# Attention, mixture of experts and GLU on one core: who makes the rests of the split weights, and where the first GLU conversions stand

## The chip, the core and the metric

The kernel runs on one core of a Trainium2 chip. The metric is the device time of one execution in microseconds; less is better. The engines of the core are TensorE (PE, with its weight loads as PEld), VectorE (DVE), ScalarE (ACT), GpSimd (POOL) and SyncE (SP, which here only issues transfers). Each has its own queue and works through it in order; they wait for each other by semaphores.

## The reference

Three stages, each on the output of the one before. 1536 tokens (2 sequences of 768, model width 512).

```python
# 1. attention: 8 heads of 64, a window of 128 keys and 4 sink keys
scores = where(is_sink | in_window, q @ k.T / sqrt(D), -1e9)
x = softmax(scores) @ v
# 2. mixture of 8 experts, one per token, at most 384 tokens each
logits = x @ w_gate
e = argmax(logits, axis=1);  g = softmax(logits)[n, e]
x[n] = g * (relu(x[n] @ w1[e]) @ w2[e])      # 0 where the expert was full
# 3. GLU, d_ff 1536
out = (sigmoid(x @ w_gate2) * (x @ w_val)) @ w_out
```

## The kernel before

Every product of stages 2 and 3 is made at float32 accuracy from two parts of each operand: a high part (the operand rounded to the PE's fp32r format) and a rest (operand minus high part). A product is then three matmuls: high by high, high by rest, rest by high. Weights arrive by DMA in one of four `stage` buffers of 128 x 2048 and are turned into a `pair` (high part and rest). For an expert's weights this is `split_w` (L127 to 132): ACT casts the high part (L131), an engine `eng` subtracts (L132, 128x1024). An expert has 8 such blocks. For the GLU the weights come as 18 blocks of 1 MB in a format of two interleaved words per element, every second column of the stage, which `conv_a` first turns into float32: ACT scales (L149), DVE does a shift and two merges (L150, L152, L156). Then `conv_b` makes the pair: ACT casts (L163), `eng` subtracts (L164). A block is converted in two halves of 128x512. There are 30 GLU loads, since not all 18 blocks fit at once.

The order of every engine's instructions is the order in which the code issues them (the schedule is manual).

Attention works on 12 tiles of 128 tokens and ends in a list of steps by hand (L618 to 627) for the last tile. In it `keep(n)` (L485 to 489) issues n matmuls whose product nobody reads, in a PSUM bank of pool `ps_v`; they keep PE running. `keep(8)` stands there ahead of `logits`, `keep(32)` (L632) behind the last count of tokens (L631). `place` forms a token's position in its expert (L438, L440, L447; its running count is L442 on POOL), `scatter` writes its row (L468).

`experts` goes over the 8 experts. Each has a main tile of 128 tokens (48 matmuls at L754 in four runs of 12, with transposes L725 and L764 and evacuations on ACT and DVE: xh L728 and xl, hr L758, hh L767 and hl L768, yr L773) and extra tiles (`more_tiles`) that run only when the expert has more than 128 or 256 tokens, under `tc.If` (L818, L820). In this data experts 0 and 7 have two extra tiles, 3 and 5 one, the others none. `split_next` splits one block of a later expert and issues the next load (SP, L124); of the 8 of an expert four rests are made by POOL (`G_`) and four by DVE (`V`). From the end of expert 1 to that of expert 6, `order_ids` (L682 to 684) has POOL issue two indirect scatters that write the order of the tokens to DRAM. At the end of expert 7, before its extra tiles, `whole` and `convert` make the first two GLU blocks; blocks 2 and 3 follow after the last `put_y` and the zeros of the unused columns of yh and yl (L893, L894).

`glu` works on three chunks of 512 tokens (the last one 416 wide here), each in 12 steps. Step t does, in order: `conv_a` of up to four half blocks, `up` (24 matmuls at L167 to L169 into two banks, ACT's sigmoid L961 after the first 12, DVE's product L962, gh by ACT L963, gl by DVE L965), `conv_b` of those half blocks and the loads that follow, and `down` of step t - 1 (12 matmuls into the accumulators, from gh and gl). Of the 28 half blocks that are left at the start, step 0 takes four and the next ones three each; those of the 12 reloaded blocks follow by the same rule in the last two chunks.

Of the kernel before, what the change touches and what calls it, by code (L numbers as in the profile page):

```python
# [1 line left out]

# [17 lines left out]
P = 128  # L20
# [5 lines left out]
def kernel(  # L26
# [145 lines left out]
    def attention():  # L172
        with ExitStack() as st:
# [87 lines left out]
            def scores(n):  # L261
# [7 lines left out]
                t = i % NT  # L269
                ps = [ps_s.tile([P, BW + P], F32, tag="s", name="s") for _ in range(4)]  # L270
                for p in range(2):
# [212 lines left out]

            def keep(n):  # L485

                idle = ps_v.tile([P, 512], F32, tag="pv", name="idle")
                for _ in range(n):
                    nc.tensor.matmul(idle, ones, ones.unsqueeze(1).to_broadcast([P, 4, P]), start=True, stop=True)
# [128 lines left out]
            for f, *a in (  # L618
                (recip, j, 1), (divide, j, 1, 0, D + E), (transposes, n - 1, 0), (turned, n - 1, 0),
                (transposes, n - 1, 1), (turned, n - 1, 1), (sink_T, i), (pv, n - 2), (sink_pv, n - 2),  # L620
                (logits, j), (best, j), (where, j), (onehot, j), (pv, n - 1),
                (gate, j, 0), (place, j), (gate, j, 1), (gate, j, 2), (scatter, j),
                (sink_pv, n - 1), (recip, i, 0), (recip, i, 1), (divide, i, 0, D, D + E), (divide, i, 1, D, D + E),
                (keep, 8), (logits, i), (divide, i, 0, 0, D), (best, i), (where, i), (onehot, i),
                (divide, i, 1, 0, D), (gate, i, 0), (gate, i, 1), (gate, i, 2), (place, i), (scatter, i),
            ):
                f(*a)
# [65 lines left out]
    def experts(yh, yl):  # L693
        with ExitStack() as st:
# [99 lines left out]

            def more_tiles(e):

                w1a, w1b, w2a, w2b = (weights(4 * e + x) for x in range(4))

                def one(j):
                    x = turn_x(xe[:, j - 1], 1)  # L800
                    u = bank(ps_u, 1)
                    go(products(u, x, w1a, True, True))
                    ra = relu(u)
                    u = bank(ps_u, 1)
                    b = products(u, x, w1b, True, True)
                    go(b[:6])
                    ha = turn_h(ra, 0)
                    go(b[6:])
                    rb = relu(u)
                    y = bank(ps_y, 1)  # L810
                    a = products(y, ha, w2a, True, False)
                    go(a[:6])
                    hb = turn_h(rb, 1)
                    go(a[6:])
                    go(products(y, hb, w2b, False, True))
                    return raw_y(y, 1)

                with tc.If(cnt_e[e] > P):  # L818
                    put_y(e, 1, one(1))
                    with tc.If(cnt_e[e] > 2 * P):  # L820
                        put_y(e, 2, one(2))

            V, G_ = nc.vector, nc.gpsimd
            xs = {0: load_x(0), 1: load_x(1)}
# [5 lines left out]
            for e in range(E):  # L830
                w1a, w1b, w2a, w2b = (weights(4 * e + j) for j in range(4))
                m = 8 * e
                if e:
                    load_x_next(e + 2)
                    load_more(e)
                    split_next(m + 2, G_)
                    split_next(m + 3, V)
# [3 lines left out]
                if e:  # L841
                    put_y(e - 1, 0, yr)
                    split_next(m + 4, G_)
                else:
# [14 lines left out]
                if e:  # L859
                    split_next(m + 6, G_)  # L860
                if e + 1 < E:
# [8 lines left out]
                if e:  # L870
                    split_next(m + 8, G_)
                    split_next(m + 9, V)
                elif e == 0:
                    cnt_e = counts([nc.tensor.engine, nc.scalar.engine, nc.vector.engine])
                go(products(y, hb, w2b, False, True))
                yr = raw_y(y, 0)
                if e == 0:
                    pi = order(hp)
                elif e < 7:
                    order_ids(pi, 2 * (e - 1), 2 * e)  # L880
                if e + 1 == E:
                    for g in range(2):
                        whole(g)
                        convert(g)
                more_tiles(e)
            load_ids()
# [7 lines left out]
            nc.vector.tensor_copy(out=yl[:, :, bass.ds(kept, P)], in_=z)  # L894
            for g in range(2, 4):
                whole(g)
                convert(g)

    def whole(q):
        for step in range(3):  # L900
            conv_a([(q, 0, 512), (q, 512, SUB)], step)

    def convert(q):
        for h in range(2):
            conv_b(q, q, h * 512, h * 512 + 512, nc.gpsimd)
        load_glu(q + 4, q)


    def glu(yh, yl):
        with ExitStack() as st:  # L910
# [105 lines left out]
            def run(t0, t1, w, half, before):  # L1016
# [6 lines left out]
                for t in range(t0, t1):  # L1023
                    pend = []
                    n, r = steps[t]
                    while half and len(pend) < 4:
                        x, h = half[0]
                        if todo[x][0] > n + 2 or len(pend) == 3 and todo[x][0] > n + 1:
                            break
# [6 lines left out]
                    for x, h in pend:  # L1036
                        conv_b(x % 4, todo[x][2], h * 512, h * 512 + 512, nc.gpsimd)
                        if h and x + 4 < len(todo):
# [130 lines left out]
```

## Time and profile before

| what | value |
|---|---|
| median of 3 runs | 703.72 us (701.37 to 704.37) |
| profiled execution | 700.3 us |
| its span in the trace | 698.6 us |
| PE busy | 620.9 us, 89% |
| DVE busy | 377.2 us, 54% |
| ACT busy | 305.8 us, 44% |
| POOL busy | 273.1 us, 39% |
| mean granted clock of PE | 0.958 |

Stages by the trace: attention to about 136 us, its tail and the order to about 150, experts to 376, GLU to the end. The shares are means over the whole span; what bounds a stage is read in that stage. The rows below are from the timelines (start, duration, engine, line, operation, what is written and read, count; in brackets the idle time of that engine just before and what ended it) and from tables over short windows. PE's durations of single matmuls overlap, so their distance is their cost.

### The profile page before, as it was taken

How to read it: one execution, taken by the hardware profiler on the slowest of the kernel's cores; microseconds unless marked ns; L12 is line 12 of the kernel's file. 1: busy time of each engine (PE TensorE's matmuls, PEld its weight loads, DVE VectorE, ACT ScalarE, POOL GpSimd, SP SyncE). 2: the span in 40 equal slices, each digit the busy share in tenths (PEclk: the TensorE clock that was granted, in tenths of full speed). 3: DMA queues.
4: the chain of work that ended last, by engine and by line, in shares of the span. 5: the costliest groups of instructions: out<-in, count | busy, mean ns of one | idle time of the engine just before them, and what ended most of it. 6: DMA issues, size and time to landing. Idle time of an engine off the chain costs nothing.

```text
span 698.6 us, 9497 instructions
## 1 busy us (share of the span) xinstructions
PE 620.9 (89%) x3316; PEld 504.7 (72%) x3316; DVE 377.2 (54%) x784; ACT 305.8 (44%) x590; POOL 273.1 (39%) x250
## 2 busy tenths in 40 slices
PE   7899899899896998999497688989999999799896
PEld 4888788757674776776376566767888887789784
DVE  2565655542177526547415999994217951128921
ACT  3567666512286546566323553452214521124321
POOL 3145867540079617638301543452102420203422
PEclk9999879999999999999799999999999999899998
DMA  6977966050067929729700444544001340101101
GB/s 161 296 216 249 318 177 202 21 192 33 0 195 256 241 96 273 240 64 227 284 1 7 164 136 176 181 142 161 30 31 40 141 182 4 44 20 61 61 0 66
DMA packets 43640, 94.09 MB, mean 135 GB/s; under 512 B 5664, under 2 KB 24352, under 8 KB 39728
## 3 DMA queue, kind: packets, MB, share of 16 engines
q1 hardware_dynamic: 41264, 87.10, 41.0%
q0 software_dynamic: 2304, 6.09, 2.3%
q8 instruction: 38, 0.62, 0.4%
q14 instruction: 34, 0.28, 0.1%
HBM read 82.63 MB, written 10.75 MB: 134 GB/s over the span
## 4 chain that ended last, share of the span: by engine, by line
PE 28%; issue 11%; DVE 8%; ACT 5%; POOL 1%; POOLq 0%; ACTq 0%; DVEq 0%
PE g L167 5%; PE g L168 5%; PE g L169 5%; PE u L754 5%; DVE stage L152 3%; DVE stage L156 3%; PE acc L167 3%; PE acc L169 3%; PE acc L168 3%; ACT stage L149 2%; ACT pair L163 2%; DVE g L962 1%; ACT gh L963 1%; DVE stage L150 0%; ACT g L961 0%
## 5 line engine op out<-in xcount | busy, mean ns | idle before, releaser
L164 POOL TENSOR_TENSOR pair<-stage,pair 128x512 fp32r<-128x512 f32 x60 | 88.3, 1499 | 179.1 <-ACT pair L163 139.9
L132 POOL TENSOR_TENSOR pair<-stage,pair 128x1024 fp32r<-128x1024 f32 x37 | 93.4, 2527 | 88.4 <-ACT pair L131 88.2
L167 PE MATMUL g<-yh,pair 128*128 128x512 f32 (+1 forms) x288 | 110.2, 383 | 7.9 <-issue 4.8
L168 PE MATMUL g<-yl,pair 128*128 128x512 f32 (+1 forms) x288 | 110.0, 382 | 0.0
L169 PE MATMUL g<-yh,pair 128*128 128x512 f32 (+1 forms) x288 | 109.7, 381 | 0.0
L754 PE MATMUL u<-pair,xh 128*128 128x512 f32 x224 | 64.6, 416 | 25.1 <-ACT xh L728 14.2
L963 ACT CAST gh<-g 128x512 fp32r<-128x512 f32 (+1 forms) x36 | 21.3, 593 | 131.6 <-DVE g L962 127.6
L962 DVE TENSOR_TENSOR g<-g,g 128x512 f32<-128x512 f32 (+1 forms) x36 | 23.4, 649 | 90.2 <-PE g L169 85.8
L754 PEld LDWEIGHTS u<-pair,xh 128*128 128x128 f32 x224 | 41.9, 196 | 38.6 <-ACT xh L728 15.9
L167 PE MATMUL acc<-pair,gh 128*128 128x512 f32 x132 | 53.9, 408 | 17.4 <-ACT gh L963 17.4
L132 DVE TENSOR_TENSOR pair<-stage,pair 128x1024 fp32r<-128x1024 f32 x27 | 59.1, 2187 | 17.0 <-ACT pair L131 16.7
L167 PEld LDWEIGHTS g<-yh,pair 128*128 128x128 f32 x288 | 55.1, 191 | 17.3 <-issue 5.2
L131 ACT CAST pair<-stage 128x1024 fp32r<-128x1024 f32 x64 | 65.3, 1050 | 4.2 <-PEq L818 2.5
L754 PE MATMUL u<-pair,hh 128*128 128x512 f32 x224 | 61.0, 400 | 1.6 <-ACT pair L131 1.4
L168 PEld LDWEIGHTS g<-yl,pair 128*128 128x128 f32 x288 | 55.2, 192 | 8.0
L169 PEld LDWEIGHTS g<-yh,pair 128*128 128x128 f32 x288 | 55.2, 192 | 7.8
L295 ACT ACTIVATE pt<-sc,neg 128x260 f32<-128x260 f32 (+1 forms) x96 | 44.6, 491 | 34.4 <-DVE neg L284 34.3
L152 DVE SCALAR_TENSOR_TENSOR stage<-stage 128x512 int32<-128x512 int32 x60 | 57.5, 1009 | 3.3 <-ACT stage L149 3.2
L150 DVE TENSOR_SCALAR stage<-stage 128x512 int32<-128x512 int32 x60 | 55.9, 987 | 0.0
L169 PE MATMUL acc<-pair,gl 128*128 128x512 f32 x132 | 53.9, 408 | 0.0
L168 PE MATMUL acc<-pair,gh 128*128 128x512 f32 x132 | 52.8, 400 | 0.0
L754 PEld LDWEIGHTS u<-pair,hh 128*128 128x128 f32 x224 | 40.8, 188 | 13.9 <-ACT pair L131 4.6
(157 smaller groups left out, 1034.6 us busy)
## 6 DMA issues: line engine op xcount, KB each, us to landing
stage<-in_we_dram SPq DMA_DIRECT2D x64, 512.0 KB, 6.5
stage<-in_wd_dram SPq DMA_DIRECT2D x30, 1024.0 KB, 4.9
vraw<-in_vr_dram SPq DMA_DIRECT2D x12, 288.0 KB, 6.4
vt<-in_vt_dram SPq DMA_DIRECT2D x12, 256.0 KB, 3.3
kraw<-in_kd_dram SPq DMA_DIRECT2D x22, 132.0 KB, 4.6
qraw<-in_qd_dram SPq DMA_DIRECT2D x22, 128.0 KB, 4.2
slots<-zero SPq DMA_DIRECT2D x1, 2048.0 KB, 9.3
xs<-slots SPq DMA_DIRECT2D x8, 256.0 KB, 4.4
```

The source lines that it names most:

```text
L131: nc.scalar.copy(out=t[:, 0], in_=raw)
L132: eng.tensor_sub(out=t[:, 1], in0=raw, in1=t[:, 0].bitcast(F32))
L150: nc.vector.tensor_scalar(out=l_, in0=l_, scalar1=29, scalar2=None, op0=ALU.logical_shift_right)
L152: nc.vector.scalar_tensor_tensor(out=l_, in0=h_, scalar=3, in1=l_, op0=ALU.logical_shift_left, op1=ALU.bitwise_or)
L164: eng.tensor_sub(out=slot[s][:, 1, n0:n1], in0=f, in1=h_.bitcast(F32))
L167: nc.tensor.matmul(ps, ah, bh, start=start, stop=False)
L168: nc.tensor.matmul(ps, ah, bl, start=False, stop=False)
L169: nc.tensor.matmul(ps, al, bh, start=False, stop=stop)
L295: nc.scalar.activation(out=pt_[i][:, h, :w], in_=scs_[n][j][:, :w], func=AF.Exp, scale=-1.0, bias=neg_[i][:, h:h + 1],)
L754: nc.tensor.matmul(ps, a, b, start=start, stop=stop)
L962: nc.vector.tensor_tensor(out=g, in0=g, in1=pss[1], op=ALU.mult)
L963: nc.scalar.copy(out=gh[:, :w], in_=g)
```

## The change

Four things change.

1. All rests of weights in the experts and the GLU are made by DVE; POOL keeps ten rests in attention, the zeros of yl, the scatters of the order and the output.
2. In expert 7 only GLU block 0 is converted ahead of the extra tiles. The halves of blocks 1 to 3 and the pair of block 1 are put between the operations of the extra tiles, one at a time, at four places of each tile, in the list `fills`; where an extra tile is not run, an Else branch does them. The pairs of blocks 2 and 3 follow the zeros as before. Blocks 4 and 5 are loaded earlier.
3. `keep(8)` ahead of `logits` becomes `keep(9)` directly behind the last `sink_pv`, writing to a bank of `ps_s`, where the scores were.
4. A GLU step takes at most three half blocks.

```diff
-            def keep(n):
-
-                idle = ps_v.tile([P, 512], F32, tag="pv", name="idle")
+            def keep(n, pool=None):
+
+                if pool is None:
+                    idle = ps_v.tile([P, 512], F32, tag="pv", name="idle")
+                else:
+                    idle = ps_s.tile([P, 512], F32, tag="s", name="idle")
...
-                (keep, 8), (logits, i), (divide, i, 0, 0, D), (best, i), (where, i), (onehot, i),
+                (sink_pv, n - 1), (keep, 9, ps_s), (recip, i, 0), (recip, i, 1),
...
-            def more_tiles(e):
+            def more_tiles(e, fills):
...
+                    def beside():
+                        for f in todo[:1]:
+                            f()
+                        del todo[:1]
+
                     x = turn_x(xe[:, j - 1], 1)
                     u = bank(ps_u, 1)
                     go(products(u, x, w1a, True, True))
+                    beside()
                     ra = relu(u)
...
+                n = 4 * (len(fills) + 1) // 8
+                with tc.If(cnt_e[e] > P) as more:
+                    put_y(e, 1, one(1, fills[:n]))
+                    with tc.If(cnt_e[e] > 2 * P) as most:
+                        put_y(e, 2, one(2, fills[n:]))
+                    if fills:
+                        with most.Else():
+                            rest(fills[n:])
+                if fills:
+                    with more.Else():
+                        rest(fills)
...
-                    split_next(m + 2, G_)
+                    split_next(m + 2, V)
...
+                fills = []
                 if e + 1 == E:
-                    for g in range(2):
-                        whole(g)
-                        convert(g)
-                more_tiles(e)
+                    whole(0, 0, SUB)
+                    convert(0)
+                    load_glu(4, 0)
+                    for q in range(1, 4):
+                        fills += [partial(whole, q, h * 512, h * 512 + 512) for h in range(2)]
+                        if q == 1:
+                            fills.append(partial(convert, 1))
+                more_tiles(e, fills)
+            load_glu(5, 1)
...
-                    while half and len(pend) < 4:
+                    while half and len(pend) < 3:
                         x, h = half[0]
-                        if todo[x][0] > n + 2 or len(pend) == 3 and todo[x][0] > n + 1:
+                        if todo[x][0] > n + 2:
                             break
...
-                        conv_b(x % 4, todo[x][2], h * 512, h * 512 + 512, nc.gpsimd)
+                        conv_b(x % 4, todo[x][2], h * 512, h * 512 + 512, nc.vector)
```

The order of instructions in the queues shows the moves. First DVE in a GLU step of the first chunk, before:

```order
L962 TENSOR_TENSOR g<-g,g_5041 128x512
L965 TENSOR_TENSOR gl<-g,gh 128x512
L150 TENSOR_SCALAR stage_82<-stage_82 128x512 x2
L150 TENSOR_SCALAR stage_83<-stage_83 128x512
L152 SCALAR_TENSOR_TENSOR stage_82<-stage_82 128x512 x2
L152 SCALAR_TENSOR_TENSOR stage_83<-stage_83 128x512
L156 SCALAR_TENSOR_TENSOR stage_82<-stage_82 128x512 x2
L156 SCALAR_TENSOR_TENSOR stage_83<-stage_83 128x512
L962 TENSOR_TENSOR g<-g,g_5096 128x512
```

And DVE in such a step after (L991 is the product, L994 the low part, L165 the rest, L151, L153 and L157 the conversion):

```order
L991 TENSOR_TENSOR g<-g,g_5078 128x512
L994 TENSOR_TENSOR gl<-g,gh 128x512
L165 TENSOR_TENSOR pair_88<-stage_80,pair_88 128x512 x2
L165 TENSOR_TENSOR pair_88<-stage_81,pair_88 128x512
L151 TENSOR_SCALAR stage_81<-stage_81 128x512
L151 TENSOR_SCALAR stage_82<-stage_82 128x512 x2
L153 SCALAR_TENSOR_TENSOR stage_81<-stage_81 128x512
L153 SCALAR_TENSOR_TENSOR stage_82<-stage_82 128x512 x2
L157 SCALAR_TENSOR_TENSOR stage_81<-stage_81 128x512
L157 SCALAR_TENSOR_TENSOR stage_82<-stage_82 128x512 x2
L991 TENSOR_TENSOR g<-g,g_5130 128x512
```

Three rests have come into the row between the low part and the next conversion.

ACT at the end of expert 7's main tile before, with the jump over the extra tiles and the cast of the first extra tile's xh:

```order
L773 COPY yr<-u 128x512
L149 ACTIVATE stage_80<-stage_80 128x512 x2
L163 CAST pair_86<-stage_80 128x512 x2
L149 ACTIVATE stage_81<-stage_81 128x512 x2
L163 CAST pair_86<-stage_81 128x512 x2
L818 COMPARE_AND_BRANCH
L728 CAST xh<-t 128x512
```

And after, into the first extra tile:

```order
L777 COPY yr<-u 128x512
L150 ACTIVATE stage_80<-stage_80 128x512 x2
L164 CAST pair_86<-stage_80 128x512 x2
L836 COMPARE_AND_BRANCH
L732 CAST xh<-t 128x512
L150 ACTIVATE stage_81<-stage_81 128x512
L762 ACTIVATE hr<-u 128x512
L771 CAST hh<-t 128x512
L150 ACTIVATE stage_81<-stage_81 128x512
L762 ACTIVATE hr<-u 128x512
L164 CAST pair_86<-stage_81 128x512 x2
L771 CAST hh<-t 128x512
```

The second block's four operations have moved from ahead of the jump to three places inside the tile.

POOL in the experts before, around the end of expert 1 (idsd is the order of the tokens in DRAM, pi where each goes):

```order
L132 TENSOR_TENSOR pair_84<-stage_81,pair_84 128x1024
L132 TENSOR_TENSOR pair_85<-stage_82,pair_85 128x1024
L132 TENSOR_TENSOR pair_86<-stage_83,pair_86 128x1024
L132 TENSOR_TENSOR pair_87<-stage_80,pair_87 128x1024
L684 DMA idsd<-ids_67,pi 1536x1 x2
L818 UNCONDITIONAL_BRANCH
L132 TENSOR_TENSOR pair_88<-stage_81,pair_88 128x1024
```

And POOL after, from the last work of attention on:

```order
L651 TENSOR_TENSOR tmp<-kd_2284,lower_66 128x64
L797 CAST yl<-zeros 128x1664 x4
L721 UNCONDITIONAL_BRANCH
L688 DMA idsd<-ids_67,pi 1536x1 x3
L836 UNCONDITIONAL_BRANCH
L721 UNCONDITIONAL_BRANCH
L688 DMA idsd<-ids_67,pi 1536x1 x9
```

With the rests gone, nothing is left between the twelve scatters of the order but jumps.

## Rows read from the trace of the kernel before

**Rows 1.** Window in GLU chunk 1: length, busy per engine, PE clock, DMA share, GB/s.

```profile
410.00:420.00 10.00, 8.77 (x38) 6.64 (x37) 9.32 (x12) 4.49 (x8) 4.55 (x4) 1.00 0.44 135
```

**Rows 2.** Timeline of DVE and POOL, one GLU step of chunk 1.

```profile
434.06 0.68 DVE L962 TENSOR_TENSOR g<-g,g 128x512 f32<-128x512 f32 x1
435.42 0.69 DVE L965 TENSOR_TENSOR gl<-g,gh 128x512 fp32r<-128x512 f32 x1 [0.68 <-ACT gh L963]
436.02 4.53 POOL L164 TENSOR_TENSOR pair<-stage,pair 128x512 fp32r<-128x512 f32 x3 [5.45 <-ACT pair L163]
436.02 3.36 DVE L150 TENSOR_SCALAR stage<-stage 128x512 int32<-128x512 int32 x3
439.31 3.00 DVE L152 SCALAR_TENSOR_TENSOR stage<-stage 128x512 int32<-128x512 int32 x3
442.23 1.89 DVE L156 SCALAR_TENSOR_TENSOR stage<-stage 128x512 int32<-128x512 int32 x3
444.03 0.68 DVE L962 TENSOR_TENSOR g<-g,g 128x512 f32<-128x512 f32 x1
```

**Rows 3.** DVE lines: shortest/median/longest in ns, first and last start in us.

```profile
L150 DVE TENSOR_SCALAR stage<-stage x60: 413/988/1559, 331.3 to 656.2; 128x512 int32<-128x512 int32 x60
L152 DVE SCALAR_TENSOR_TENSOR stage<-stage x60: 677/683/1803, 333.9 to 660.0; 128x512 int32<-128x512 int32 x60
L132 DVE TENSOR_TENSOR pair<-stage,pair x27: 1224/2089/3650, 195.1 to 329.3; 128x1024 fp32r<-128x1024 f32 x27
```

**Rows 4.** Timelines of DVE and PE at the start of the GLU.

```profile
375.66 0.43 DVE L894 CAST yl<-zeros 128x512 f32 x1
...
394.44 0.80 PE L167 MATMUL acc<-pair,gh 128*128 128x512 f32 x1 [5.35 <-ACT gh L963]
```

**Rows 5.** Timeline of ACT, sigmoids of GLU steps 10 and 11, and of chunk 3.

```profile
481.41 0.60 ACT L961 ACTIVATE g<-g 128x512 f32<-128x512 f32 x1 [2.60 <-PE g L169]
489.57 0.60 ACT L961 ACTIVATE g<-g 128x512 f32<-128x512 f32 x1 [4.09 <-PE g L169]
...
616.72 0.52 ACT L961 ACTIVATE g<-g 128x416 f32<-128x416 f32 x1 [3.58 <-PE g L169]
623.72 0.52 ACT L961 ACTIVATE g<-g 128x416 f32<-128x416 f32 x1 [3.59 <-PE g L169]
...
677.30 0.52 ACT L961 ACTIVATE g<-g 128x416 f32<-128x416 f32 x1 [3.59 <-PE g L169]
```

**Rows 6.** Timelines of ACT and PE around expert 7's first extra tile.

```profile
335.85 1.28 ACT L163 CAST pair<-stage 128x512 fp32r<-128x512 f32 x2 [1.39 <-DVE stage L156]
...
342.29 0.58 ACT L728 CAST xh<-t 128x512 fp32r<-128x512 f32 x1
342.92 2.07 PE L754 MATMUL u<-pair,xh 128*128 128x512 f32 x4 [9.77 <-ACT xh L728]
```

**Rows 7.** Timelines of PE and POOL, at starts of expert tiles.

```profile
206.36 1.15 PE L754 MATMUL u<-pair,xh 128*128 128x512 f32 x4 [0.15 <-PEq L818]
209.40 1.79 POOL L684 DMA_INDIRECT idsd<-ids,pi  x1 [0.30 <-issue]
213.64 1.19 PE L754 MATMUL u<-pair,xh 128*128 128x512 f32 x4 [1.41 <-POOL pair L132]
227.11 1.01 PE L754 MATMUL u<-pair,xh 128*128 128x512 f32 x2 [4.49 <-issue]
273.93 1.29 PE L754 MATMUL u<-pair,xh 128*128 128x512 f32 x4 [3.11 <-PEq L818]
```

**Rows 8.** Window behind a scatter, columns as in rows 1.

```profile
215.00:216.00 1.00, 1.00 (x7) 0.87 (x6) 1.00 (x1) 1.00 (x2) 0.92 (x1) 1.00 0.00 0
```

**Rows 9.** Timelines of PE and POOL at the end of attention.

```profile
138.03 3.38 PE L489 MATMUL idle<-ones 128*128 128x512 bf16 x8 [1.53 <-DVE x L385]
140.55 0.21 POOL L442 TENSOR_TENSOR acc<-acc,oh_all 128x8 bf16<-128x8 bf16 x1
141.32 7.24 PE L489 MATMUL idle<-ones 128*128 128x512 bf16 x32
```

More of the change, by code (lines that the diff above doesn't have):

```diff
@@ L1 @@
 from contextlib import ExitStack
+from functools import partial
 import concourse.bass as bass
@@ L269, in scores @@
                 t = i % NT
-                ps = [ps_s.tile([P, BW + P], F32, tag="s", name="s") for _ in range(4)]
+                ps = [ps_s.tile([P, 512], F32, tag="s", name="s")[:, :BW + P] for _ in range(4)]
                 for p in range(2):
@@ L622, in attention @@
                 (gate, j, 0), (place, j), (gate, j, 1), (gate, j, 2), (scatter, j),
-                (sink_pv, n - 1), (recip, i, 0), (recip, i, 1), (divide, i, 0, D, D + E), (divide, i, 1, D, D + E),
-                (keep, 8), (logits, i), (divide, i, 0, 0, D), (best, i), (where, i), (onehot, i),
+                (sink_pv, n - 1), (keep, 9, ps_s), (recip, i, 0), (recip, i, 1),
+                (divide, i, 0, D, D + E), (divide, i, 1, D, D + E), (logits, i), (divide, i, 0, 0, D), (best, i), (where, i), (onehot, i),
                 (divide, i, 1, 0, D), (gate, i, 0), (gate, i, 1), (gate, i, 2), (place, i), (scatter, i),
@@ L793, in zero_y, with one @@
                 nc.gpsimd.tensor_copy(out=yl[:, d], in_=z)
-            def more_tiles(e):
+            def more_tiles(e, fills):
                 w1a, w1b, w2a, w2b = (weights(4 * e + x) for x in range(4))
-                def one(j):
+                def one(j, todo):
+                    def beside():
+                        for f in todo[:1]:
+                            f()
+                        del todo[:1]
                     x = turn_x(xe[:, j - 1], 1)
@@ L807, in one @@
                     ha = turn_h(ra, 0)
+                    beside()
                     go(b[6:])
                     rb = relu(u)
+                    beside()
                     y = bank(ps_y, 1)
@@ L813, in one @@
                     hb = turn_h(rb, 1)
+                    beside()
                     go(a[6:])
@@ L816, in one, with rest @@
                     return raw_y(y, 1)
[L818 to L823, printed above, removed]
+                def rest(todo):
+                    for f in todo:
+                        f()
+                n = 4 * (len(fills) + 1) // 8
[9 more added lines that the diff above has]
+                        rest(fills)
+            V = nc.vector
             xs = {0: load_x(0), 1: load_x(1)}
@@ L842, in experts @@
                     put_y(e - 1, 0, yr)
-                    split_next(m + 4, G_)
+                    split_next(m + 4, V)
                 else:
@@ L859, in experts @@
                 if e:
-                    split_next(m + 6, G_)
+                    split_next(m + 6, V)
                 if e + 1 < E:
@@ L870, in experts @@
                 if e:
-                    split_next(m + 8, G_)
+                    split_next(m + 8, V)
                     split_next(m + 9, V)
@@ L894, in experts, with whole @@
             nc.vector.tensor_copy(out=yl[:, :, bass.ds(kept, P)], in_=z)
[L895 to L899, printed above, removed]
+            for q in range(2, 4):
+                convert(q)
+                load_glu(q + 4, q)
+    def whole(q, n0, n1):
         for step in range(3):
-            conv_a([(q, 0, 512), (q, 512, SUB)], step)
+            conv_a([(q, n, n + 512) for n in range(n0, n1, 512)], step)
     def convert(q):
         for h in range(2):
-            conv_b(q, q, h * 512, h * 512 + 512, nc.gpsimd)
-        load_glu(q + 4, q)
+            conv_b(q, q, h * 512, h * 512 + 512, nc.vector)
     def glu(yh, yl):
```

## The prediction

> **What bounds the kernel now.** I read the page's busy shares and 40 slices first. TensorE (PE) is busy for 89% of the span and its clock is close to full in most slices, so there is little to win except where it stands still, and I looked for those places with the timelines. They lie in three stretches.
>
> The GLU's first chunk is the largest. In ten of its microseconds PE is busy 8.77 and VectorE (DVE) 9.32, at a granted clock of 1.00 [rows 1]. One step there [rows 2] is a closed ring on DVE: its product L962 starts at 434.06 and again at 444.03, 9.97 us later, and between the two it is never idle except 0.68 us before L965. PE is not that slow: from step 10 on, with no half block left to convert, the sigmoid L961 starts at 481.41 and next at 489.57, so a full step (24 matmuls up, 12 down) takes 8.16 us, or 0.227 us a matmul [rows 5]. PE therefore loses 1.8 us a step as long as conversions run, 28 half blocks at three a step, some nine steps. In the ring the two conversion lines L150 and L152 take 3.3 and 2.9 us for three halves [rows 2]; over the whole run their shortest are 413 and 677 ns, the longest 1559 and 1803 [rows 3]. They are long exactly while GpSimd (POOL) makes its three rests at L164, 436.02 to 440.55; L156, which follows when POOL has finished, takes 0.60 a piece. I read that as POOL stretching DVE.
>
> The second place is the last expert: PE waits 9.77 us, to 342.92, for xh, which ScalarE (ACT) casts at 342.29 only after converting two GLU blocks [rows 6]. The third are waits of 0.15 to 4.49 us at the experts' ends [rows 7]. In chunk 2 I count no gain.
>
> **The change, part by part.** Sums are made on the profiled execution (700.3 us), which lies 3.4 below the median of the runs.
>
> *GLU, rests on DVE.* Removed: three L164 a step on POOL. Added on DVE, between the low part L965 and L150 of the next halves: three subtractions of 128x512. None is in the trace; the nearest is L965, the same operation and shape on DVE, 0.60 from its start to L150's [rows 2]. If L150 and L152 fall to what they take undisturbed, the ring is 1.36 (L962 to L965) + 0.60 + 3 x 0.60 rests + 3 x 0.41 + 3 x 0.60 + 3 x 0.60 = 8.6 us, against PE's 8.16. The bounds of a ring: 8.2, where PE sets it, and 9.97 + 1.80 = 11.8, where the stretch stays. I take 8.6, since L156, right behind in the same ring, already shows the undisturbed pace.
>
> What 8.6 costs depends on the slack at the start. Before, gh of step 0 came so late that PE waited 5.35 until 394.44; its second up was finished at 389.09 [rows 4]. Behind the zeros of yl (375.66 + 0.4, [rows 4]) DVE now has four rests (2.4) and three halves (4.8 by the costs above): 383.3, and with 0.8 for the rests' waits on ACT's casts L962 at about 384.1; gh is cast by 385.5, 3.6 before PE wants it. The ring falls back 0.44 a step over 9.3 steps, 4.1 in all. That is about the slack, so I count no wait. PE unhindered from 389.09 reaches the sigmoid of step 10 after 9 downs of 2.72, 8 ups of 5.44 and half an up, at 459.8; in the trace it starts at 481.41 [rows 5]. Gain **21.6**. In chunk 3 (416 columns) a step without a wait takes 7.00 (616.72 to 623.72), and the last 7 steps, 623.72 to 677.30, take 53.58 for 49.0 [rows 5]. There a ring of 8.3 to 8.6 is slower than PE by 1.3 to 1.6 a step, but over four steps with new halves only, which the steps ahead cover. Gain **4.6**, bounds 0 and 4.6.
>
> *Expert 7.* ACT converts block 0 alone ahead of the extra tiles; its two casts (1.28) start at 335.85, so xh can follow at 337.1 instead of 342.29 [rows 6]. Gain **5.1**. The six half blocks that go between the operations of two extra tiles take 1.6 us on DVE and 0.6 on ACT each. Each tile keeps PE some 12 us (48 matmuls of 0.227 and the transposes) and DVE and ACT have three short evacuations in it, so I cost the fills at nothing. If a fill stood ahead of the evacuation that PE needs it would cost up to 1.6, five times, 8; then the expert's gain is gone.
>
> *Experts' rests on DVE.* PE waited 1.41 at 213.64 for a rest of POOL's [rows 7]: gain **1.4**. 27 of these rests on DVE had a median of 2.1 us and a minimum of 1.2 [rows 3]; with POOL silent I expect 1.2 to 1.3, so twice as many fill about the same time. Queued behind each are xl, hl and yl on DVE, and PE's products with low parts behind those. A rest waits for ACT's cast, and ACT is in order too, so no new late load appears; a stretched rest could hold hl by 1 us some six times, bound 6.
>
> *Scatters of the token order.* POOL, rid of rests, runs its twelve scatters in one row soon after the order is known, not in pairs at expert ends. Before, one stood at 209.40 [rows 7] and the loads behind it moved nothing at 215 to 216, DMA share 0.00 [rows 8]. The 4.49 before 227.11 follows that, 3.11 before 273.93 and 0.15 before 206.36 stand behind the jump over the extra tiles (PEq L818) [rows 7]. Bounds 0 to 7.7; I take the one wait of **4.5**, which the loads explain.
>
> *Idle matmuls at the end of attention.* The eight waited 1.53 for a bank that DVE still read, ended at 141.41 and held back the position sums; POOL's sum was there at 140.76, and the 32 further ones need 7.24 [rows 9]. Placed in another bank, nine start at 136.4 and are over by 140.2. Gain **1.0** (from 140.76 instead of 141.32, and the last scatter as much earlier), bounds 0 and 2.3. Three instead of four halves in step 0 is in the slack above.
>
> Sum: 21.6 + 4.6 + 5.1 + 1.4 + 4.5 + 1.0 = 38.2, so 662.1 for the profiled execution and 703.7 - 38.2 = 665.5 for the median.
>
> **Rivals.** *The ring is 9.3, not 8.6* (each of the three rests 0.83 instead of 0.60): it falls back 1.14 a step, 10.6, and 7 of that is beyond the slack: about **673**. For it: the rests read every second word of the stage, which L965 does not. Against it: L156 reads the same stage and takes 0.60 [rows 2].
>
> *Jumps still cost.* PE, ACT and DVE now pass two new Else jumps after expert 7, and the waits at the expert ends could be the jumps' and not the loads'. The row at 273.93 names the jump for 3.11, that at 206.36 only 0.15 [rows 7]. If 4.5 stays and a new wait of 3 to 4.5 comes: **670 to 674**. The Trainium skill, "Runtime: NRT & Kernel Launch", section "Instruction fetch mechanics", states that a taken branch whose target lies outside the fetched window forces a fetch before the engine goes on; by that rule each such end pays, new ones too. By it the time is 670 to 674, by the 0.15 row 665.5; that row shows that not each jump pays here, the 3.11 row that some may.
>
> *Slower: L150 and L152 are long for another reason than POOL.* Then the rests come on top, ring 9.97 + 1.80 = 11.8: 1.8 more over nine steps is 16.8 lost in chunk 1, some 9 more where the lag runs into chunk 2, 7 in chunk 3, less the 12 of the other terms: **725**. It decides from a ring of about 11.2 on. Against it: in one ring L156 is short and it alone lies beside no rest of POOL's [rows 2].
>
> *The twelve scatters in a row delay the loads of expert 1*, as the one at 209.40 seems to have done. Twelve of 1.79 [rows 7] are 21.5 us of issue; they begin behind expert 0's main tile, and its two extra tiles, some 12 us each, lie ahead of the first rest, which stood at 195.1 [rows 3]. So they should be through; if not, some 2 to 5 us, **668 to 671**.
>
> **How the numbers follow.** Chances: forecast 0.52, longer ring 0.18, jumps 0.17, scatters or fills in the way 0.10, slower 0.03. The median is then 665.5; the range of 8 in 10 goes from 655 (all bounds of the small terms good, and a ring below PE's step: 7 to 10 more) to 681 (longer ring and jumps together). Other than by over 0.5% (3.5 us, about what a measurement of this kernel can tell from no change): faster 0.95, within it 0.02, slower 0.03.
>
> **What would show it.** Right: in chunk 1 the product's starts (L991 now) lie 8.2 to 8.7 apart, the lines that were L150 and L152 at 0.4 and 0.6 us, rests at 0.6; PE's wait for gh of 5.35 at the first down gone; xh of expert 7's extra tile near 337 less what was won ahead. Wrong: L150 and L152 still at 0.9 with POOL idle; a ring over 9; a wait of PE on xh or hh in the extra tiles behind a fill; new issue waits behind L836. If the time is over 690, the reading of POOL's part in DVE's pace has failed.

## The result and the profile after

The changed kernel takes 671.3 us in the median of its first runs (665.69 to 672.95) against 704.05 before: a ratio of 0.9526, 95% interval 0.9474 to 0.9579. Measured once more beside other kernels, it took 668.2 (six runs), ratio 0.9537 (0.9489 to 0.9586). The forecast was 665.5, range 655 to 681. The profiled execution took 665.69 us, its span 664.0, against 700.3 and 698.6. It is the fastest of its four: by the medians the change is worth 32.8 us, by the two traces 34.6.

One step of GLU chunk 1 on DVE, from the timeline, answers to [rows 2]:

```profile
400.47 0.68 DVE L991 TENSOR_TENSOR g<-g,g 128x512 f32<-128x512 f32 x1
401.84 0.69 DVE L994 TENSOR_TENSOR gl<-g,gh 128x512 fp32r<-128x512 f32 x1 [0.69 <-ACT gh L992]
402.45 1.89 DVE L165 TENSOR_TENSOR pair<-stage,pair 128x512 fp32r<-128x512 f32 x3
404.25 1.09 DVE L151 TENSOR_SCALAR stage<-stage 128x512 int32<-128x512 int32 x3
405.26 1.89 DVE L153 SCALAR_TENSOR_TENSOR stage<-stage 128x512 int32<-128x512 int32 x3
407.07 1.89 DVE L157 SCALAR_TENSOR_TENSOR stage<-stage 128x512 int32<-128x512 int32 x3
408.87 0.68 DVE L991 TENSOR_TENSOR g<-g,g 128x512 f32<-128x512 f32 x1
```

The ring is 8.40 us, from 9.97. The shift and the first merge are at their undisturbed pace, 0.34 and 0.60 a piece from start to start, and each rest costs 0.60. PE's waits for gh in the downs, 17.4 us in all before, are gone from the table of waits, which now begins with these lines (engine, line, what it waited for, us in total, times, longest):

```profile
PE u L758 <- ACT xh L732: 8.9, 7, 4.5
PE g L168 <- issue: 4.9, 1, 4.9
PE m L228 <- DMA vt<-in_vt_dram: 3.6, 1, 3.6
```

The two traces set side by side by stretches; the ends are starts of transposes and matmuls on PE, of the zeros of yl on DVE and of sigmoids on ACT:

| stretch | before | after | difference | forecast |
|---|---|---|---|---|
| start to the first transposes of expert 0 | 149.12 | 149.32 | +0.20 | -1.0 |
| to the transposes of expert 2's tokens | 49.70 | 53.15 | +3.45 | 0 |
| to expert 7's first extra tile | 133.73 | 124.94 | -8.79 | -5.9 |
| to the zeros of yl | 43.11 | 39.62 | -3.49 | -5.1 |
| to the sigmoid of GLU step 10 | 105.75 | 84.29 | -21.46 | -21.6 |
| to the sigmoid of step 24 (chunk 3) | 120.84 | 120.20 | -0.64 | 0 |
| to the sigmoid of step 35 | 79.58 | 75.14 | -4.44 | -4.6 |
| to the end | 16.77 | 17.34 | +0.57 | 0 |
| sum | 698.6 | 664.0 | -34.6 | -38.2 |

The GLU's two gains came out as summed. The largest loss against the forecast lies in expert 0, where PE twice waits for nothing that the profile shows ("issue"; such waits are called waits for instructions below). Timeline of PE there, and then a window behind it (length, busy per engine, granted clock, DMA share, GB/s):

```profile
174.90 1.20 PE L758 MATMUL u<-pair,hh 128*128 128x512 f32 x4 [0.99 <-issue]
179.24 0.65 PE L786 MATMUL t<-ident,yr 128*128 128x128 f32 x4 [1.32 <-issue]
```

```profile
180.00:186.00 6.00, 5.27 (x19) 4.03 (x17) 1.29 (x2) 1.24 (x3) 0.00 (x0) 0.72 0.00 0
```

Behind the two waits the granted clock is 0.72 in the mean of 6 us, so partly at the lower of its two levels (1.2 and 2.4 GHz). At the same time POOL issues the twelve scatters, 162.78 to 179.44, and stands still itself once, 1.84 us before 177.18.

In expert 7, PE still waits for xh, and the clock is low behind that wait as well (PE, then the window):

```profile
332.51 2.07 PE L758 MATMUL u<-pair,xh 128*128 128x512 f32 x4 [4.50 <-ACT xh L732]
```

```profile
328.00:340.00 12.00, 7.50 (x24) 5.97 (x24) 6.12 (x10) 4.23 (x8) 0.00 (x0) 0.72 0.42 157
```

### The profile page after: what moved, and what is told of

The parts are those of the page before. It is cut to its first block, busy times and chain, and to the rows that moved or that the text cites. A ratio compares the mean times of both kernels' runs of the same rounds, so it can differ in the third digit from the quotient of the medians.

```text
span 664.0 us, 9340 instructions
## 1 busy us (share of the span) xinstructions
PE 612.1 (92%) x3317; PEld 505.5 (76%) x3317; DVE 360.0 (54%) x871; ACT 305.7 (46%) x590; POOL 109.1 (16%) x163
## 4 chain that ended last, share of the span: by engine, by line
issue 27%; PE 21%; ACT 1%; DVE 1%; POOL 1%; POOLq 0%; DVEq 0%; ACTq 0%
PE u L758 4%; PE g L168 4%; PE g L170 4%; PE g L169 4%; PE acc L168 2%; PE acc L170 2%; PE acc L169 2%; POOL out_dram L1023 1%; PE t L768 0%; DVE stage L153 0%; ACT pair L132 0%; ACT yr L777 0%; ACT hh L771 0%; PE t L786 0%; DVE stage L157 0%
## 5 line engine op out<-in xcount | busy, mean ns | idle before, releaser
L1023 POOL DMA_INDIRECT out_dram<-o,ids x11 | 10.8, 978 | 467.1 <-ACT o L1039 464.7
L991 DVE TENSOR_TENSOR g<-g,g 128x512 f32<-128x512 f32 (+1 forms) x36 | 23.4, 650 | 90.3 <-PE g L170 88.3
L133 DVE TENSOR_TENSOR pair<-stage,pair 128x1024 fp32r<-128x1024 f32 x54 | 64.2, 1220 | 11.7 <-ACT pair L132 11.7
L990 ACT ACTIVATE g<-g 128x512 f32<-128x512 f32 (+1 forms) x36 | 20.5, 568 | 68.1 <-PE g L170 68.1
L170 PE MATMUL acc<-pair,gl 128*128 128x512 f32 x132 | 51.6, 391 | 0.0
L169 PE MATMUL acc<-pair,gh 128*128 128x512 f32 x132 | 51.5, 390 | 0.0
L168 PE MATMUL acc<-pair,gh 128*128 128x512 f32 x132 | 51.4, 390 | 0.0
L331 PE MATMUL pv<-v,pts 128*128 128x73 f32 x352 | 44.1, 279 | 0.0
L331 PEld LDWEIGHTS pv<-v,pts 128*128 128x128 f32 x352 | 43.7, 201 | 0.0
```

The costliest lines, as they stand in the source:

```text
L133: eng.tensor_sub(out=t[:, 1], in0=raw, in1=t[:, 0].bitcast(F32))
L168: nc.tensor.matmul(ps, ah, bh, start=start, stop=False)
L169: nc.tensor.matmul(ps, ah, bl, start=False, stop=False)
L170: nc.tensor.matmul(ps, al, bh, start=False, stop=stop)
L331: nc.tensor.matmul(pv_[n][:, h], pts_[n, h // 2][:, h % 2, j], vb[kb][:, 4 * a + h], start=(h == 0 and j == 0), stop=(h == 3 and j == len( ...
L990: nc.scalar.activation(out=g, in_=pss[0], func=AF.Sigmoid)
```

## The experiments

Each was timed beside the kernel before. Single executions of one kernel differ by up to 9 us. Behind attention, whose code hardly changed, expert 0's first transposes start between 147.3 and 153.6 in the fourteen traces. So stretches are compared here, and medians beside them. Three of them come back often: "zeros to step 10" is from the zeros of yl to the sigmoid of GLU step 10, "chunk 3" from the sigmoid of step 24 to that of step 35, and "expert 0", unless said otherwise, from its first extra tile's transposes to those of expert 2's tokens. Each stretch of an experiment is read in one execution.

**1. GLU's rests back on POOL.**

```diff
-                        conv_b(x % 4, todo[x][2], h * 512, h * 512 + 512, nc.vector)
+                        conv_b(x % 4, todo[x][2], h * 512, h * 512 + 512, nc.gpsimd)
```

> The changed kernel with the GLU's rests back on POOL and nothing else undone. Theory (POOL's rests stretch DVE's conversion lines, and that made the ring of 9.97 us): the ring in chunk 1 is again 9.9 to 10.0 us against 8.40 in the changed kernel, the first conversion line takes about 1.1 and the second about 1.0 us a piece while POOL works, and the time rises by 20 to 26 us, to about 691 to 697. Rival (the gain in the GLU came from three instead of four halves and from the earlier conversions of expert 7): the ring stays near 8.4 or below and the time within 3 us of the changed kernel's 671.3.

682.7 us, ratio to before 0.9716 (0.9672 to 0.976). DVE and POOL in one step:

```profile
386.92 0.68 DVE L991 TENSOR_TENSOR g<-g,g 128x512 f32<-128x512 f32 x1
388.89 4.53 POOL L165 TENSOR_TENSOR pair<-stage,pair 128x512 fp32r<-128x512 f32 x3 [5.45 <-ACT pair L164]
388.89 3.35 DVE L151 TENSOR_SCALAR stage<-stage 128x512 int32<-128x512 int32 x3
392.17 3.01 DVE L153 SCALAR_TENSOR_TENSOR stage<-stage 128x512 int32<-128x512 int32 x3
396.90 0.67 DVE L991 TENSOR_TENSOR g<-g,g 128x512 f32<-128x512 f32 x1
```

The ring is 9.98 again, but zeros to step 10 takes 96.84, not 105.75. With chunk 3 (79.50) the rests are worth 16.9 us, and the other 8.9 of the 21.5 in chunk 1 came from elsewhere. The median rose by 11.4, or 14.5 against the second set of runs below. So the ring is as the theory has it, but the time rose by less than its 20 to 26, and the 8.9 fit what the rival names, the earlier conversions and the three halves.

**2. Idle work on POOL.**

```diff
+                    if t < 5:
+                        for _ in pend:
+                            nc.gpsimd.tensor_sub(out=scr, in0=zero, in1=g[0].bitcast(F32))
+                    elif t < 9:
+                        nc.gpsimd.tensor_copy(out=hold[:, t:t + 1], in_=g[0][:, 0:1].bitcast(F32))
+                        for _ in range(4):
+                            nc.gpsimd.memset(scr, 0.0)
```

> The changed kernel with work on POOL that nobody needs, tied to gh of each step: in steps 0 to 4 of chunk 1 three subtractions of 128x512 that read a constant tile and gh, in steps 5 to 8 four memsets of 128x512 that read nothing. The rests stay on DVE. Theory (it is POOL's use of the memory beside DVE that stretches, whatever data it is): with the subtractions the ring in steps 0 to 4 goes from 8.40 to 10 to 12 us, since rests and the first conversion line lie beside them; with the memsets it is between 8.4 and 10, open which. Rival (before, DVE was slow because its conversions and POOL's rests met on the same stage buffers or were ordered after each other): the ring stays at 8.4 in all steps, since POOL touches no stage.

POOL subtracting beside DVE's rests, then POOL clearing beside them (timelines of both engines, two steps):

```profile
390.24 5.14 POOL L1069 TENSOR_TENSOR scr<-zero,gh 128x512 f32<-128x512 f32 x3 [6.57 <-ACT gh L994]
390.74 5.19 DVE L166 TENSOR_TENSOR pair<-stage,pair 128x512 fp32r<-128x512 f32 x3
395.85 1.09 DVE L152 TENSOR_SCALAR stage<-stage 128x512 int32<-128x512 int32 x3
...
437.75 2.27 POOL L1073 MEMSET scr<- 128x512 f32 x4
437.69 1.89 DVE L166 TENSOR_TENSOR pair<-stage,pair 128x512 fp32r<-128x512 f32 x3
439.50 1.48 DVE L152 TENSOR_SCALAR stage<-stage 128x512 int32<-128x512 int32 x3
```

With subtractions the rests take 1.70 a piece instead of 0.60 and the ring 11.7; with memsets, which read nothing, the rests keep 0.60 and only the one-input shift loses 0.4, once. POOL touched no stage, so the rival falls: it is POOL's reading beside DVE. The Trainium skill, "SBUF — State Buffer", section "SBUF: two separate sides", states that DVE and GpSimd (POOL) take a shared port of this memory in turns for whole instructions, and that a DVE instruction with two inputs from it is held up only by a GpSimd one that reads it. The trace agrees: 1.89 against 5.19 for the two-input rests. The ring beside memsets is 8.8 to 8.9. There is one execution, 686.5 us.

**3. Scatters in the GLU's first steps.**

```diff
-                elif e < 7:
-                    order_ids(pi, 2 * (e - 1), 2 * e)
...
+                    if t < 6:
+                        nc.gpsimd.tensor_copy(out=hold[:, t:t + 1], in_=g[0][:, 0:1].bitcast(F32))
+                        order_ids(pi, 2 * t, 2 * t + 2)
+                    elif t == 9:
+                        load_ids()
```

> The changed kernel with the twelve scatters of the token order taken out of expert 0 and put into steps 0 to 5 of GLU chunk 1, two a step, each pair held by a small copy that reads gh; the load of the order follows in step 9. Theory (the scatters in a row cost 3.5 us in expert 0: PE's two waits of 0.99 and 1.32 us for instructions and the stretch at a granted clock of 0.72 behind them): these waits and the slow stretch are gone, expert 1's first transposes start 3.5 us earlier, the time falls by 2 to 4 us to about 668; the scatters may show again as instruction waits in the GLU. Rival (the waits are the jumps' or the profiled execution's own): they stay at the same places, time within 1 us of the changed kernel.

668.8 us, ratio 0.9531 (0.9493 to 0.9569). Expert 0 takes 35.77 us (39.31 in the changed kernel, 35.84 before). In all traces it takes 35.7 to 35.8 wherever no scatter stands in it (seven), and 35.8, 37.6, 37.7, 38.2, 39.3, 39.9 and 41.8 with the row of twelve. So the row costs 0 to 6 us, mostly 2 to 4. But here the scatters hold up weights (DVE, step 2):

```profile
386.52 0.43 DVE L152 TENSOR_SCALAR stage<-stage 128x512 int32<-128x512 int32 x1 [3.20 <-DMA stage<-in_wd_dram]
```

Zeros to step 10 takes 92.79 instead of 84.29. By the stretches more is lost than won; by the medians the kernel is no different from the changed one, so the expected 668 came about otherwise than expected.

**4. Block 0 as a fill, too** (block 3 becomes one fill instead of two, which is not shown here).

```diff
-                    whole(0, 0, SUB)
-                    convert(0)
-                    load_glu(4, 0)
+                    fills = [partial(whole, 0, 0, SUB), partial(convert, 0)]
...
+            load_glu(4, 0)
             load_glu(5, 1)
```

> The changed kernel with GLU block 0, too, converted between the operations of expert 7's extra tiles, so that ACT has nothing ahead of the first extra tile's cast of xh. The load of block 4 follows the tiles. Theory (the remaining 4.50 us wait of PE at 332.51 is block 0's conversion, and the slow clock of 0.63 and 0.81 behind it is the wait's): the wait falls to about 0.7, the slow stretch goes with it, the GLU starts 4 to 6 us earlier, time about 666. Rival (what ACT and DVE no longer do ahead, they do inside the tiles at PE's expense, or the GLU's first step waits for block 4): the start of the GLU moves by less than 2 us, or PE waits in step 1 for gh as before.

660.0 us, ratio 0.9374 (0.9316 to 0.9432), PE and the same window:

```profile
332.89 1.20 PE L758 MATMUL u<-pair,xh 128*128 128x512 f32 x4 [0.72 <-ACT xh L732]
```

```profile
330.00:342.00 12.00, 11.28 (x56) 9.13 (x55) 7.21 (x13) 6.57 (x12) 0.00 (x0) 1.00 0.31 109
```

The first extra tile, from its transposes to the next tile's, takes 14.64 instead of 21.32, with the clock at 1.00, and zeros to step 10 is 84.28 as without it. The gain is 6.7 us: 3.8 of wait and 2.9 of clock and order behind it. By the medians it is 11.3, or 8.2 against the second set of runs; expected were 4 to 6.

**5. Scatters back in pairs.**

```diff
+                    nc.gpsimd.tensor_copy(out=hold[:, e:e + 1], in_=yr[:, 0:1])
                     order_ids(pi, 2 * (e - 1), 2 * e)
```

> The changed kernel with the twelve scatters back in pairs at the ends of experts 1 to 6, each pair held by a small copy on POOL that reads yr of that expert; rests stay on DVE. Theory (a scatter holds up what comes after it in the queues, a row of twelve holds up PE's instructions in expert 0): expert 0, from its first extra tile to the transposes for expert 2, takes 35.8 to 36 us as before the change, not 39.3; in experts 2 to 6 instruction waits of PE of 2 to 4 us come back as in rows 7, so that the time is within 3 us of the changed kernel's 671.3. Rival (the row of twelve is no cost, the waits belong to the jumps): expert 0 stays at 38 to 39 us, and the later experts don't change.

671.5 us, ratio 0.9544 (0.9501 to 0.9586). As expected, expert 0 is back at 35.74, the time is that of the changed kernel, and PE waits again where it did in [rows 7], at 227.11:

```profile
228.74 1.65 PE L759 MATMUL u<-pair,xl 128*128 128x512 f32 x3 [3.61 <-issue]
```

From the transposes of expert 2's tokens to those of expert 4's it takes 34.05 us, 35.77 before, 29.39 in the changed kernel. Moving the scatters thus won 4.7 there and lost 3.6 in expert 0. The scatters are not the whole of the first: with the pairs in place (four traces) PE waits 3.6 to 4.5 us for instructions there, but without them (ten) still 0.8 to 2.4 in seven, and not at all for over 0.3 in three.

**6. Half the experts' rests back on POOL** (`G_` for m + 2, 4, 6 and 8).

```diff
-                    split_next(m + 2, V)
+                    split_next(m + 2, G_)
```

> The changed kernel with four of the eight rests of each expert back on POOL; the scatters then stand between them as before. Theory: this part of the change is worth little, 1 to 6 us: PE waits for POOL's rests again (2.0 us in all before), rests of DVE go from 1.2 to 2.1 us, the instruction waits of experts 2 to 4 return, and expert 0's 3.5 us are won back; time 670 to 676. Rival (DVE, slowed by POOL, held PE in all experts, and this part carried the gain of the experts): over 678.

673.0 us, ratio 0.957 (0.9527 to 0.9613). PE waits 2.6 us for POOL's rests and 4.2 once for instructions; DVE's rests have a median of 2091 ns again, 1220 in the changed kernel. Set against experiment 5, which has the scatters in the same places, the three stretches between token transposes in which neither waits for instructions are longer by 1.8, 0.3 and 1.2 us: 3.3 for the rests. Of that 2.0 is PE's waits for them. From expert 2's transposes to expert 7's first extra tile the two take the same (129.6 and 129.9), because waits for instructions differ by as much the other way, and the medians can't tell them apart. The expected 670 to 676 held.

**7. No fills** (blocks 0 and 1 whole ahead of the tiles, 2 and 3 whole behind the zeros).

```diff
+                    for q in range(2):
+                        whole(q, 0, SUB)
+                        convert(q)
+                        load_glu(q + 4, q)
```

> The changed kernel with GLU blocks 0 and 1 converted whole ahead of expert 7's extra tiles, blocks 2 and 3 behind the zeros, as before the change; rests on DVE. Theory (part of the gain that was counted for the GLU's rests belongs to the conversions that left its start): PE's wait for the first extra tile's xh goes from 4.5 back to about 9 us, DVE's first product in the GLU comes about 14 us after the zeros, not 8.2, PE waits for gh of step 0 by some 3 us, and the ring's lag is no longer covered; together 10 to 13 us, time 681 to 684. Rival (only the wait ahead of the tile counts, the GLU's start is covered): 4 to 5 us, time about 676.

670.2 us, ratio 0.9524 (0.948 to 0.9567). By the median nothing is lost, so both expectations missed the time. By stretches 8.4 us are: expert 7's first extra tile takes 25.60 instead of 21.32, the rest up to the zeros 0.6 less, zeros to step 10 88.97 instead of 84.29. PE's wait for xh is 9.0 and DVE's first product comes 14.3 after the zeros, as expected, but PE waits only 1.2 for gh of step 0, not 3. The other side is that this execution lost nothing in expert 0 (35.77 us, although its scatters stand in a row) and began it at 148.7. Why none of its four runs shows the loss is open; two sets of runs of the changed kernel differ by 3 us themselves.

**8. Idle matmuls as before.**

```diff
-                (sink_pv, n - 1), (keep, 9, ps_s), (recip, i, 0), (recip, i, 1),
+                (keep, 8), (logits, i), (divide, i, 0, 0, D), (best, i), (where, i), (onehot, i),
```

> The changed kernel with keep(8) ahead of logits in the old bank, as before the change. Theory (the bank's wait held back the last tile's position sums): the idle matmuls wait again 1.5 us for DVE's read of the bank, and from the start of the last full tile's products to the first transposes of expert 0 it takes 19.7 us as before, not 18.3; the total moves by 1 to 1.5 us, less than the runs scatter, so the trace decides. Rival (the last scatter's landing sets the end, whatever the idle matmuls do): 18.3 stays.

669.6 us, ratio 0.9555 (0.9496 to 0.9615): no difference by the medians. From the last tile's sink transposes to the last scatter it takes 10.17 us, 8.68 in the changed kernel; to the first transposes of expert 0 it takes 16.24, against 15.49 and, in the second trace of the changed kernel, 17.18. In the expectation's own measure that is 19.1, against 18.3 and 20.0: the last scatter bears the theory out, the end of the tail decides nothing.

**9. Block 0 as a fill and scatters in GLU steps 7 to 9** (experiment 4's diff, the scatters taken out of expert 0 as in experiment 3, and)

```diff
+                    if 7 <= t < 10:
+                        nc.gpsimd.tensor_copy(out=hold[:, t:t + 1], in_=g[0][:, 0:1].bitcast(F32))
+                        order_ids(pi, 4 * t - 28, 4 * t - 24)
+                    elif t == 11:
+                        load_ids()
```

> The changed kernel with block 0 converted inside the extra tiles too, and the scatters in steps 7 to 9 of GLU chunk 1, four a step, where no load is urgent any more; the load of the order in step 11. Theory (the two gains are independent: 6.7 us in expert 7, 3.5 in expert 0 and up to 2 in the experts behind, and at this place the scatters hold up no weight): 654 to 658, below the 660.0 of block 0 alone. Rival (the scatters cost as much wherever they stand, or the output of chunk 1 waits for the order): 660 to 664.

656.8 us, ratio 0.9346 (0.9293 to 0.9399), inside the expectation and below both kernels; it is the shortest median, though its interval overlaps those of experiments 4 and 12. Expert 0 takes 35.77, the first extra tile of expert 7 14.63, zeros to step 10 85.41.

**10. The kernel before with only the GLU's rests on DVE.**

```diff
-                        conv_b(x % 4, todo[x][2], h * 512, h * 512 + 512, nc.gpsimd)
+                        conv_b(x % 4, todo[x][2], h * 512, h * 512 + 512, nc.vector)
```

> The kernel before with one word changed: the rests of the half blocks converted in the GLU's steps are made by DVE; experts, fills, scatters, idle matmuls and four halves in step 0 stay. Theory (the ring by itself): the ring goes from 9.97 to 8.40 us, from the zeros of yl to the sigmoid of step 10 it takes some 89 to 91 us against 105.8 before, chunk 3 gains 4.4, so 19 to 21 us in all, 683 to 685. Rival (without the shorter start DVE stays the bound and the gain of the ring is given back to waits): under 12 us, over 692.

687.6 us, ratio 0.9823 (0.9762 to 0.9883). Zeros to step 10 takes 92.73 and chunk 3 75.13, so 13.0 + 4.5 = 17.5 us by the trace and 14.7 by the medians: between the two expectations. PE still waits 5.4 us for gh of step 0. The rests of GLU blocks 0 to 3, made ahead of the steps, are still POOL's here.

**11. The changed kernel again**, unchanged.

> The changed kernel as it is, for a second look at its stages. Theory (the stages repeat, and executions differ in attention's slow stretches and in a few instruction waits of PE): from the zeros of yl to step 10 again 84.3 us, ring 8.40, chunk 3 75.1; the first transposes of expert 0 start anywhere between 148 and 153 us, expert 0 loses 0 to 3.5 us to its scatters; median 668 to 672. Rival (the gain in the GLU itself varies): one of those GLU stretches differs by over 1 us.

668.2 us (664.2 to 669.0). Zeros to step 10 is 84.28, chunk 3 75.08: the GLU's two stretches repeat to 0.1 us. Expert 0 takes 39.90, 4.1 above its time without scatters, somewhat more than expected.

**12. Idle matmuls in the gap** (experiment 9, and)

```diff
+            keep(7)
             nc.tensor.matmul(m, ones, acc[0], start=True, stop=True)
-            keep(32)
+            keep(23)
```

> As the kernel with block 0 as a fill and the scatters in GLU steps 7 to 9, and with seven of the idle matmuls moved ahead of the last count of tokens, where PE waits 2.0 us for POOL's sum, so that 23 are left behind it, not 32. Theory (since the change the tail of attention ends with the 32 idle matmuls, 7.07 us, or 8.75 where the granted clock fell behind that wait, and no longer with the arrival of the tokens): from the last tile's sink transposes to the first transposes of expert 0 it takes 14.7 to 15.0 us instead of 15.5 or 17.2, PE waits a little for the tokens again, and the clock does not fall in the idle matmuls; median 654 to 656 against 656.8. Rival (the tokens' arrival is what sets the end): 15.4 or more.

657.5 us, ratio 0.9379 (0.9335 to 0.9423), no different from experiment 9, so the expected 654 to 656 did not come. The tail itself did what the theory says: 14.64 from the sink transposes to expert 0's first ones. PE in experiment 11, a window of it, and then PE in this one:

```profile
144.24 0.17 PE L635 MATMUL m<-acc,ones 128*128 128x8 bf16 x1 [1.98 <-POOL acc L443]
```

```profile
146.00:148.00 2.00, 2.00 (x6) 0.68 (x5) 0.32 (x3) 0.00 (x0) 0.52 (x1) 0.50 0.29 111
```

```profile
143.20 0.17 PE L637 MATMUL m<-acc,ones 128*128 128x8 bf16 x1 [0.45 <-POOL acc L444]
143.22 5.12 PE L494 MATMUL idle<-ones 128*128 128x512 bf16 x23
149.28 0.63 PE L731 MATMUL t<-ident,xs 128*128 128x128 f32 x4 [0.93 <-DMA xs<-slots]
```

From the last scatter to the first transposes it takes 5.97 us, against 6.81 or 8.50 in the two traces of the changed kernel. What the tail won went again behind it: from expert 0's first transposes to the next ones (expert 1's tokens) it takes 9.07 us, 7.43 to 7.48 in all other traces. There PE had waited 0.93 for the tokens and 0.80 for xh, and from 153 to 155 the granted clock is 0.50, the lower level.

## Why the prediction was right, and where it was not

**POOL stretches DVE: right, shown** by experiments 1 and 2. The ring of 8.6 measured 8.40; the term of the shift, 0.41 a piece, is 0.34 from start to start.

**The 21.6 of chunk 1: the size right (21.46), its name wrong.** It was booked on the rests. Zeros to step 10 with and without each part says otherwise: 105.75 before, 92.73 with only the steps' rests moved (experiment 10), 96.84 with all but these (1), 84.29 with both. The steps' rests give 13 and the shorter start 9, and 13.0 + 8.9 = 21.9 is about the whole: they add. The start is again more than one thing. Without the fills alone it is 88.97 (7), so the fills give 4.7; the other 3.8, up to experiment 10's 92.73, lie with step 0's three halves instead of four and with DVE making the rests of blocks 0 to 3, and no run parts these two. The working held the start (its four rests and three halves, 384.1) but did not price it apart: a ring only counts once the slack ahead of it is known, and the start makes the slack. DVE's first product was forecast 8.4 after the zeros and came at 8.2 (367.03 to 375.26), 17.4 before.

**Chunk 3: right**, 4.44 against 4.6, and 4.45 in experiment 10.

**Expert 7: mis-sized**, 3.5 against 5.1. The wait fell by 5.27, as summed, but the first tile behind it, with fills in it, took 1.2 more, part of it at a low clock, and the second one 0.6, of which 0.3 is a wait for hl behind a fill. The fills had been costed at nothing. The larger thing was not seen: block 0 had no reason to stay ahead of the tile, and taking it along gives 6.7 more.

**Experts' rests: too small.** 1.4 was the longer of PE's two waits for them; the other, 0.6, was left out (2.0 in the table of waits). Experiments 5 and 6 show 3.3 in the stretches that can be compared.

**Scatters: the step that failed.** "So they should be through" is true of the loads: the last scatter ends at 179.44, the next weight loads go out at 199.10. What the row went with was PE's waits for instructions beside it, 0 to 6 us in expert 0. The fourth rival had the place and about the size, and the wrong carrier. The 4.5 taken for expert 2 was right in size (4.7), but its reason, that the loads explain the wait, was not. [rows 7] names no wait for a weight there, and in the idle time just before 227.11 the transfers of the kernel before ran at 410 GB/s (columns as in [rows 1]; PE's busy time is 0.00):

```profile
224.00:226.00 2.00, 0.00 (x0) 0.00 (x0) 1.22 (x1) 0.66 (x1) 1.70 (x2) 1.00 1.03 410
```

**Attention's tail: half right.** The last scatter goes out 1.5 to 2.3 us earlier, but the 32 idle matmuls became the bound, and after the 2 us wait for POOL's sum they ran 7.07 or 8.75 us. Against the kernel before that is 1.4 won or 0.3 lost, against experiment 8, which undoes this edit alone, 0.8 won or 0.9 lost. The 1.0 was no sum either: the two times that it names lie 0.56 apart.

**Jumps: the new ones show no cost** (PE's wait for the zeros of yh, 3.1, is as before), the old one over the extra tiles keeps 0.2 to 3.0, and differently in each execution. So the second rival's waits are real, and only the additional ones didn't come. The longer ring and the slower rival fell with the ring of 8.40.

**The sum: partly luck.** By the traces it missed by only 3.6 us because misses in both directions met: attention, expert 0, expert 7 and the end fell 6.8 short together, the stretch from expert 2 to expert 7 and chunk 2 gave 3.5 more than forecast.

What stays open: waits for instructions of up to 3 us that come and go between executions, why experiment 7's loss doesn't show in its median, and why the traces give the GLU's rests 16.9 or 17.5 us and the medians 11.4 to 14.7.

## What to carry to other kernels

Where an instruction's longest time is far above its shortest, see which engine works beside it, before looking at shares: POOL was busy 39% and made 1% of the chain that ended last, and taking its rests away shortened the ring of another engine. Split a gain over the edits by undoing each one, since a sum can be right and its names wrong. Work that is due later goes between the operations of a stage where its engines idle, all of it, and side transfers such as the order's scatters go where they hold up neither weights nor PE.

## What was not expected of the hardware

- POOL's scatters of 128 indices each, 1.28 us apart, go with waits of PE and of POOL itself for instructions of 0.8 to 2.0 us a time, at a DMA share of 0.05 or less in stretches of 4 to 7 us. In expert 0 that it is the scatters is shown by moving them (3, 5 and 9), though one of seven traces with the row has no such wait; by what way they do it is not.
- Behind a wait of PE of 2.0 us the clock fell in some executions only: of ten traces with the changed tail of attention, five show 7.07 us for the 32 idle matmuls and five 8.75, with a granted clock of 0.50 in a stretch of experiment 11 and 1.00 in the changed kernel's first trace.
- A DVE instruction with two inputs took 1.70 us beside a subtraction on POOL and 0.60 beside a memset.
